# Softmax denominators written into the next pair's score bank, and the packed units' masks made one unit later, in an attention and MLP kernel

## The chip, the cores and the metric

One core of one Trainium2 chip. The metric is the device time of one execution in microseconds; lower is better. The core's engines run side by side, each with its own queue of instructions in a fixed order: PE (matmul), DVE (vector), ACT (activation), POOL (GpSimd) and SP, which here only issues DMAs. They wait for one another through semaphores.

## The reference, cut to what matters

Attention with a sliding window of 128 keys and 4 sink keys over 4 batches, 8 heads, 768 positions and 64 dimensions a head, then a two-layer MLP over all 3,072 tokens. `n_sink` and `window` come as 64-bit integers, the MLP's weights as 64-bit floats.

```python
scores = scale * np.matmul(q, k.transpose(0, 1, 3, 2))
keep = is_sink | in_window
scores = np.where(keep, scores, -1000000000.0)
scores = scores - np.max(scores, axis=-1, keepdims=True)
a = np.exp(scores)
a = a / (np.sum(a, axis=-1, keepdims=True) + 1e-09)
x = np.matmul(a, v)                      # then heads side by side
h = x @ w_in
out = np.maximum(0.01 * h, h) @ w_out
```

## The kernel before, in words

The tokens are cut into 8 units of 384 (half a batch each). A unit's attention runs by pairs of heads (4 pairs), a pair by blocks of 128 queries (j = 0, 1, 2). The first two units ("native") handle two heads side by side; the other six ("packed") one head at a time, with other masks. The unit's MLP has 16 steps: 12 matmuls into a bank h (`h<-xh,wih` and two more kinds), an activation, then 9 matmuls into three banks o. Each product is made in three parts, from high and low halves: `gh` and `gl` of the activation, `wih`/`wil` and `woh`/`wol` of the weights, `xh`/`xl` of attention's output.

The order of PE's instructions is written by hand: attention is a stream of small pieces, the MLP another, and a table of due pieces interleaves them. The first unit's attention (35 pieces and its start) runs ahead of any MLP work; from then on unit u+1's attention goes between unit u's MLP steps. DVE, ACT, POOL and SP get their order from a list scheduler at build time, which works with its own estimates of time; on the chip the order is fixed, whatever the real times are.

For a native pair, block j does this. PE writes the scores of the two heads into two banks (L296, tiles `s`). DVE takes the masked maximum and writes the shifted scores to SBUF (L308, `pk`, and `negm`); ACT makes the exponentials and their sums (L310, `pk` and `sm`); POOL copies the sink columns (L458, `sk`). Two blocks later PE transposes `pk` into a bank t (L337) and ACT, or DVE for the very first pair, copies it out (L342, `pt`). After three blocks `spread` makes the reciprocals of the sums: DVE adds 1e-9 into spare columns of a score bank (L320), takes the reciprocal out of it (L321), and POOL spreads it over 64 columns (L324, `rb`). Three blocks later (two for the first unit's last pair) `gather` transposes the sinks and `rb` into one bank (L372, L375), which is copied out (L379, `r`); `values` multiplies with V and with the sinks (L392, L398, bank `acc`) and DVE scales the result (L404, `r`). `xh` and `xl` follow (L405, L406).

Score banks: in the first unit the tags s0, s1, o0, o1 go round, so a block's two banks come back two blocks later; from the second unit on only s0 and s1 are left, and every block uses both: the first head's scores go to s0, the second's to s1. A bank is written again only when every reader of its last tile is done, the spare columns' reader included.

The MLP's weights arrive as 64-bit words. For each of the 16 steps DVE decodes an input and an output block with three instructions each (L185, L187, L189, through bank d, tiles `di`/`wi` and `do`/`wo`), ACT rounds it to the high half (L198), POOL subtracts for the low half (L199). The first three steps' weights are decoded during the first unit's attention, the block for step n+3 during step n of the first unit's MLP. In that unit the steps' banks h are the same bank, but for step 1. `wi`, `wo` and two mask tiles (`sel`, `own_rows`) share a ring of three buffers.

`late_masks` (L112) makes the masks that only packed units read, mostly on POOL (L119 to L140), with L136 and L142 on DVE; `whole_limits` (L101) makes the 64-bit limits with three DVE instructions (L106 to L108) that only the last part of the program reads. Before, both are written in the first unit's pair 2, block 0.

Of the kernel before, what the change touches and what calls it, by code (L numbers as in the profile page):

```python
# [147 lines left out]
def fast_path(ctx, tc, cpool, qp, qk, vu, vs, vt, wq, out, ident, lims, wz, negm, wmin, wmax):  # L148
# [68 lines left out]
    def native(u):  # L217
        return u < NATU
# [86 lines left out]
    def soft(u, h, j, w, src, mask, sm):  # L305
        col = (u * H + h) * T + j
        neg = negm[:, col:col + 1]
        anchor[0] = nc.vector.tensor_tensor_reduce(out=w, in0=src, in1=mask, scale=-SCALE, scalar=3.0e38,  # L308
                                                   op0=ALU.add, op1=ALU.min, accum_out=neg)
        nc.scalar.activation(out=w, in_=w, func=AF.Exp, scale=-1.0, bias=neg, accum_out=sm)  # L310
# [6 lines left out]
    def spread(u, pair, state, ps):  # L317
        sm = state["sm"]
        rest = ps[:, SPARE:SPARE + 2 * T].rearrange("p (j h) -> p j h", j=T)
        nc.vector.tensor_scalar(out=rest, in0=sm, scalar1=1e-9, scalar2=None, op0=ALU.add)  # L320
        nc.vector.reciprocal(out=sm, in_=rest)  # L321
        rb = xpool.tile([P, TU], F32, tag="rb", name=f"rb{u}_{pair}", bufs=1)
        rb = rb.rearrange("p (c d) -> p c d", c=2 * T)
        nc.gpsimd.tensor_copy(out=rb, in_=sm.rearrange("p j h -> p (j h)").rearrange("p (c o) -> p c o", o=1)  # L324
                              .broadcast_to([P, 2 * T, D]))
        state["rb"] = rb
# [90 lines left out]
        return (u, pair + 1) if pair < NPAIR - 1 else (u + 1, 0)  # L417

    count = [0]

    def attend(u, pair, pend):
        state = {"sk": sks[pair % 2]}
        nxt = ahead(u, pair)

        def later(lag, f, join=False):
            pend.append((count[0] + lag, f, join))

        def fetch(o):
            more = nxt[0] < NU
            if native(u) and native(nxt[0]) and nxt not in raws:  # L430
                load_pair(*nxt)
            if more and o == 0:
                load_values(*nxt)
            if not native(u) and o == 0:
                load_head(u, 2 * pair + 1)
            elif more and not native(nxt[0]):
                load_head(nxt[0], 2 * nxt[1])

        def tile_pt():
            if "pt" not in state:  # L440
                state["pt"] = apool.tile([P, 2, 2 * TU], F32, tag="pt", name=f"pt{u}_{pair}", bufs=1)

        def pt_then(f, *args):
            tile_pt()
            f(*args)

        if native(u):
            state["sm"] = apool.tile([P, T, 2], F32, tag="sm", name=f"sm{u}_{pair}")
            sp = raws.pop((u, pair))
            for j in range(T):  # L450
                kn = KSL[u % 2][j][1]
                pss = scores(u, pair, j, (0, 1), sp)
                w = apool.tile([P, 2, W3], F32, tag="pk", name=f"pk{u}_{pair}_{j}", bufs=3)
                a = P if kn == W3 else 0
                for o, ps in enumerate(pss):
                    soft(u, 2 * pair + o, j, w[:, o, 0:kn], ps[:, 0:kn], masks[min(T * (u % 2) + j, 2)],
                         state["sm"][:, j, o:o + 1])
                    nc.gpsimd.tensor_copy(out=state["sk"][:, 0, j, o, :], in_=w[:, o, a:a + NSK])  # L458
                if j == 0:
                    fetch(0)  # L460
                    if native(nxt[0]):
                        load_sinks(*nxt)
                    if u == 0 and pair == 0:
                        rest(anchor[0])
                    if u == 0 and pair == 2:
                        whole_lim.append(whole_limits(tc, cpool, lim_raw, lim_lo, anchor[0]))
                        late.append(late_masks(tc, cpool, iopool, masks, anchor[0]))
                count[0] += 1
                if j == T - 1:
                    spread(u, pair, state, pss[1])  # L470
                later(LAGT, lambda j=j, w=w: pt_then(turn_native, u, pair, j, w, state))
                yield
        else:
            for o in range(2):
                h = 2 * pair + o
                sp = split_head(u, h)
                fetch(o)
                (split_sinks if o else load_sinks)(u, pair)
                w = apool.tile([P, 2 * W3], F32, tag="pk", name=f"pk{u}_{h}", bufs=3)
                w = w[:, 0:T * W1].rearrange("p (j k) -> p j k", j=T)  # L480
                sm = apool.tile([P, T], F32, tag="sm", name=f"sm{u}_{h}")
                for j in range(T):
                    ps, = scores(u, pair, j, (o,), sp)
                    if KSL[u % 2][j][1] == W3:
                        nc.vector.copy_predicated(out=ps[:, W1:W3], mask=late[0][1], data=ps[:, 0:P])  # L485
                        src = ps[:, P:W3]
                    else:
                        src = ps[:, 0:W1]
                    soft(u, h, j, w[:, j], src, late[0][0][min(T * (u % 2) + j, 2)], sm[:, j:j + 1])
                    count[0] += 1  # L490
                    if j == T - 1:
                        nc.vector.tensor_scalar(out=sm, in0=sm, scalar1=1e-9, scalar2=None, op0=ALU.add)
                        nc.vector.reciprocal(out=sm, in_=sm)
                        nc.vector.tensor_tensor(out=w, in0=w, in1=sm.rearrange("p (j o) -> p j o", o=1)
                                                .broadcast_to([P, T, W1]), op=ALU.mult)
                        sk, sinks = state["sk"], w[:, :, 0:NSK]
                        nc.gpsimd.tensor_copy(out=sk[:, 0:3:2, 0:T, o, :].bitcast(F32R),
                                              in_=sinks.rearrange("p (r j) s -> p r j s", r=1)
                                              .broadcast_to([P, 2, T, NSK]))
                        nc.gpsimd.tensor_tensor(out=sk[:, 1, 0:T, o, :], in0=sinks, in1=sk[:, 0, 0:T, o, :],  # L500
                                                op=ALU.subtract)
                        later(LAGT, lambda o=o, w=w: pt_then(turn_packed, u, pair, o, w, state))
                    yield
        last = u == 0 and pair == NPAIR - 1
        if native(u):
            later(LAGT if last else LAGG, lambda: gather(u, pair, state))
        later(LAGT if last else LAGV if native(u) else LAGP, lambda: values(u, pair, state), not native(u))
# [125 lines left out]
    for x, _ in enumerate(mlp_stream()):  # L633
        u, r = divmod(x, mlp_steps)
# [216 lines left out]
```

## Time and profile before

| what | value |
|---|---|
| median of 3 runs | 702.59 us (701.48 to 704.52) |
| the profiled execution | 702.91 us, span 701.1 us |
| PE busy | 687.3 us, 98% of the span |
| DVE busy | 446.1 us, 64% |
| POOL busy | 321.0 us, 46% |
| ACT busy | 318.8 us, 45% |
| chain that ended last | PE 93%, DVE 3%, DMA 1%, ACT 1% |
| granted clock of PE | 0.999 |

The busy shares are averages over unlike stretches: the first 37 us hold the first unit's attention alone, and the MLP fills PE from then on. [...]

### The profile page before, as it was taken

How to read it: one execution, taken by the hardware profiler on the slowest of the kernel's cores; microseconds unless marked ns; L12 is line 12 of the kernel's file. 1: busy time of each engine (PE TensorE's matmuls, PEld its weight loads, DVE VectorE, ACT ScalarE, POOL GpSimd, SP SyncE). 2: the span in 40 equal slices, each digit the busy share in tenths (PEclk: the TensorE clock that was granted, in tenths of full speed). 3: DMA queues.
4: the chain of work that ended last, by engine and by line, in shares of the span. 5: the costliest groups of instructions: out<-in, count | busy, mean ns of one | idle time of the engine just before them, and what ended most of it. 6: DMA issues, size and time to landing. Idle time of an engine off the chain costs nothing.

```text
span 701.1 us, 11524 instructions
## 1 busy us (share of the span) xinstructions
PE 687.3 (98%) x3950; PEld 597.8 (85%) x3950; DVE 446.1 (64%) x1183; ACT 318.8 (45%) x827; POOL 321.0 (46%) x442
## 2 busy tenths in 40 slices
PE   8899999999999999999999999999999999999996
PEld 5577788988888988888898888888888889889995
DVE  5997887655656665565566565556566565377772
ACT  4865566444454444444444444444444444222221
POOL 4676688544444543543444454354344444122220
PEclk9999999999999999999999999999999999999999
DMA  6666556222123111222113221221222320068751
GB/s 223 207 223 197 192 204 202 82 66 69 47 72 108 56 43 61 60 85 69 58 53 106 70 57 47 62 91 44 67 73 53 110 74 33 1 218 277 252 169 48
DMA packets 29535, 74.14 MB, mean 106 GB/s; under 512 B 3488, under 2 KB 9120, under 8 KB 29472
## 3 DMA queue, kind: packets, MB, share of 16 engines
q1 hardware_dynamic: 29184, 73.10, 32.0%
q8 instruction: 32, 0.52, 0.3%
q14 instruction: 31, 0.25, 0.1%
q10 hardware_dynamic: 288, 0.26, 0.1%
HBM read 67.06 MB, written 6.29 MB: 105 GB/s over the span
## 4 chain that ended last, share of the span: by engine, by line
PE 93%; DVE 3%; DMA 1%; ACT 1%; issue 0%; SPq 0%; ACTq 0%; DVEq 0%
PE h L549 38%; PE o L586 37%; PE acc L392 6%; PE s L301 5%; PE t L348 3%; PE s L296 2%; PE t L337 1%; DVE pk L308 1%; DMA qkraw<-in_qk 1%; PE acc L398 1%; DMA qkn<-in_qp 1%; PE acc L388 1%; PE t L350 0%; ACT pk L310 0%; DVE ob L599 0%
## 5 line engine op out<-in xcount | busy, mean ns | idle before, releaser
L568 POOL TENSOR_TENSOR gl<-g,gh 128x384 fp32r<-128x384 f32 x127 | 129.9, 1023 | 276.2 <-ACT gh L567 260.8
L549 PE MATMUL h<-xh,wih 128*128 128x384 f32 x512 | 180.8, 353 | 0.0
L549 PE MATMUL h<-xl,wih 128*128 128x384 f32 x512 | 172.7, 337 | 0.0
L549 PE MATMUL h<-xh,wil 128*128 128x384 f32 x512 | 172.7, 337 | 0.0
L586 PE MATMUL o<-woh,gh 128*128 128x512 f32 (+1 forms) x400 | 153.5, 385 | 0.2 <-DVE ob L599 0.2
L586 PE MATMUL o<-wol,gh 128*128 128x512 f32 (+1 forms) x400 | 152.8, 385 | 0.0
L310 ACT ACTIVATE pk<-pk,negm 128x132 f32<-128x132 f32 (+1 forms) x192 | 81.6, 426 | 96.7 <-DVE negm L308 96.3
L559 ACT ACTIVATE g<-h 128x384 f32<-128x384 f32 x127 | 62.0, 488 | 123.7 <-PE h L549 103.4
L586 PE MATMUL o<-woh,gl 128*128 128x512 f32 (+1 forms) x400 | 113.8, 387 | 0.0
L549 PEld LDWEIGHTS h<-xh,wih 128*128 128x128 f32 x512 | 96.4, 188 | 4.0 <-issue 2.2
L549 PEld LDWEIGHTS h<-xl,wih 128*128 128x128 f32 x512 | 96.6, 189 | 0.4 <-POOL xl L406 0.2
L549 PEld LDWEIGHTS h<-xh,wil 128*128 128x128 f32 x512 | 96.1, 188 | 0.0
L567 ACT CAST gh<-g 128x384 fp32r<-128x384 f32 x128 | 65.7, 513 | 65.4 <-DVE g L566 64.8
L566 DVE TENSOR_TENSOR g<-h,g 128x384 f32<-128x384 f32 x127 | 69.9, 550 | 35.0 <-ACT g L559 34.9
L586 PEld LDWEIGHTS o<-woh,gl 128*128 128x128 f32 x400 | 74.0, 188 | 17.1 <-POOL gl L568 0.4
L586 PEld LDWEIGHTS o<-woh,gh 128*128 128x128 f32 x400 | 75.1, 188 | 12.0 <-DVE ob L599 0.9
L586 PEld LDWEIGHTS o<-wol,gh 128*128 128x128 f32 x400 | 75.1, 188 | 11.0
L485 DVE COPY_PREDICATED s<-tri,s 128x128 f32<-128x128 int8 x120 | 35.0, 292 | 53.8 <-PE s L301 51.9
L262 POOL TENSOR_TENSOR qksp<-qkraw,qksp 64x396 fp32r<-64x396 f32 (+1 forms) x48 | 56.4, 1176 | 23.1 <-POOL gl L568 18.6
L301 PEld LDWEIGHTS s<-qksp 128*128 128x128 f32 x288 | 53.5, 188 | 8.6
L301 PE MATMUL s<-qksp 128*128 128x260 f32 (+1 forms) x288 | 56.3, 277 | 0.0
L261 ACT CAST qksp<-qkraw 128x780 fp32r<-128x780 f32 (+1 forms) x48 | 43.2, 901 | 25.2 <-PE s L301 22.2
(114 smaller groups left out, 853.8 us busy)
## 6 DMA issues: line engine op xcount, KB each, us to landing
craw<-in_wq SPq DMA_DIRECT2D x32, 512.0 KB, 4.1
qkraw<-in_qk SPq DMA_DIRECT2D x24, 454.0 KB, 3.2
qkraw<-in_qk SPq DMA_DIRECT2D x24, 390.0 KB, 3.0
wiraw<-in_wq SPq DMA_DIRECT2D x16, 512.0 KB, 4.2
woraw<-in_wq SPq DMA_DIRECT2D x16, 512.0 KB, 3.7
out<-ob SPq DMA_DIRECT2D x23, 256.0 KB, 2.0
v<-in_vu SPq DMA_DIRECT2D x16, 256.0 KB, 2.6
v<-in_vu SPq DMA_DIRECT2D x16, 192.0 KB, 2.4
```

What stands on the lines that cost most here:

```text
L261: nc.scalar.copy(out=sp[:, 0:TU + n], in_=raw[:, 0:TU + n])
L262: nc.gpsimd.tensor_tensor(out=sp[D:P, TU:TU + n], in0=raw[D:P, TU:TU + n], in1=sp[D:P, TU:TU + n].bitcast(F32), op=ALU.subtract)
L301: nc.tensor.matmul(pss[0][:, 0:kn], lhsT=sp[:, off + j * P:off + (j + 1) * P], rhs=sp[:, TU + k0:TU + k0 + kn], start=c == 0, stop=c == 1)
L310: nc.scalar.activation(out=w, in_=w, func=AF.Exp, scale=-1.0, bias=neg, accum_out=sm)
L392: nc.tensor.matmul(acc[o * D:(o + 1) * D, qo:qo + m], lhsT=vv[:, kb * P + o * D:kb * P + (o + 1) * D], rhs=state["pt"][:, o, po:po + m], s ...
L485: nc.vector.copy_predicated(out=ps[:, W1:W3], mask=late[0][1], data=ps[:, 0:P])
L549: nc.tensor.matmul(ph[:, 0:TU], lhsT=w[:, cs], rhs=x, start=cc == 0 and c == 0, stop=cc == NCC - 1 and c == 2)
L559: nc.scalar.mul(g, ph[:, 0:TU], 0.01)
L566: anchor[0] = nc.vector.tensor_tensor(out=g, in0=ph[:, 0:TU], in1=g, op=ALU.max)
L567: nc.scalar.copy(out=gh, in_=g)
L568: (nc.vector if step == NU * NFC - 1 else nc.gpsimd).tensor_tensor(out=gl, in0=g, in1=gh.bitcast(F32), op=ALU.subtract)
L586: nc.tensor.matmul(acc, lhsT=(gl if c == 2 else gh)[:, t * P:(t + 1) * P], rhs=(wl if c == 1 else wh)[:, cols], start=f == 0 and c == 0, s ...
```

## The change

`spread` is no longer run when a native pair's last block is written. It waits in a list, and the next pair's block 0 runs it after its own maxima, with its own second bank for the spare columns (or, behind the second unit, the first packed head's first bank). `whole_limits` and `late_masks` are written in the second unit's pair 1, block 0.

```diff
--- before.py
+++ after.py
@@ -417,6 +417,7 @@
         return (u, pair + 1) if pair < NPAIR - 1 else (u + 1, 0)
 
     count = [0]
+    waiting = []
 
     def attend(u, pair, pend):
         state = {"sk": sks[pair % 2]}
@@ -457,17 +458,19 @@
                          state["sm"][:, j, o:o + 1])
                     nc.gpsimd.tensor_copy(out=state["sk"][:, 0, j, o, :], in_=w[:, o, a:a + NSK])
                 if j == 0:
+                    if waiting:
+                        waiting.pop()(pss[1])
                     fetch(0)
                     if native(nxt[0]):
                         load_sinks(*nxt)
                     if u == 0 and pair == 0:
                         rest(anchor[0])
-                    if u == 0 and pair == 2:
+                    if u == 1 and pair == 1:
                         whole_lim.append(whole_limits(tc, cpool, lim_raw, lim_lo, anchor[0]))
                         late.append(late_masks(tc, cpool, iopool, masks, anchor[0]))
                 count[0] += 1
                 if j == T - 1:
-                    spread(u, pair, state, pss[1])
+                    waiting.append(lambda ps: spread(u, pair, state, ps))
                 later(LAGT, lambda j=j, w=w: pt_then(turn_native, u, pair, j, w, state))
                 yield
         else:
@@ -487,6 +490,8 @@
                     else:
                         src = ps[:, 0:W1]
                     soft(u, h, j, w[:, j], src, late[0][0][min(T * (u % 2) + j, 2)], sm[:, j:j + 1])
+                    if waiting:
+                        waiting.pop()(ps)
                     count[0] += 1
                     if j == T - 1:
                         nc.vector.tensor_scalar(out=sm, in0=sm, scalar1=1e-9, scalar2=None, op0=ALU.add)
```

The program's order on PE is the same instruction for instruction up to the branch that is not taken. On the others it moves, since the scheduler lays them out anew. Three places follow. In the names, `pk_p_j` is pair p, block j; `s_h_j` head h, block j; the unit's number is left out, the last number only counts tiles. A matmul or DVE step on two heads has two rows, and `negm` is the second half of each L308.

First place, DVE, first unit, pair 1, block 1. Before:

```order
L308 ISA pk_1_1_221,negm<-s_2_1_217,m_95 128x260
L308 ISA negm 128x1
L320 TENSOR_SCALAR s_1_2_168<-sm_0_134 128x6
L321 RECIPROCAL sm_0_134<-s_1_2_168 128x6
L308 ISA pk_1_1_221,negm<-s_3_1_218,m_95 128x260
L308 ISA negm 128x1
```

After:

```order
L308 ISA pk_1_1_221,negm<-s_2_1_217,m_95 128x260
L308 ISA negm 128x1
L320 TENSOR_SCALAR s_3_0_186<-sm_0_134 128x6
L308 ISA pk_1_1_221,negm<-s_3_1_218,m_95 128x260
L308 ISA negm 128x1
L321 RECIPROCAL sm_0_134<-s_3_0_186 128x6
```

The sum and reciprocal of pair 0 stood in bank `s_1_2` (tag s1), which `s_3_1` writes next; they now stand in `s_3_0` (tag o1), which `s_3_2` writes next, and the reciprocal has gone behind the second head's maximum.

Second place, DVE, second unit, pair 0, block 1. Before:

```order
L185 TENSOR_SCALAR di_516<-wiraw_511 128x512
L308 ISA pk_0_1_555,negm<-s_0_1_551,m_96 128x260
L308 ISA negm 128x1
L187 SCALAR_TENSOR_TENSOR di_516<-wiraw_511,di_516 128x512
L308 ISA pk_0_1_555,negm<-s_1_1_552,m_96 128x260
L308 ISA negm 128x1
L189 SCALAR_TENSOR_TENSOR wi_515<-wiraw_511,di_516 128x512
L404 TENSOR_TENSOR r_3_574<-acc_3_576,r_3_574 128x384
```

After, from the second head of block 0 on:

```order
L308 ISA pk_0_0_468,negm<-s_1_0_465,m_96 128x260
L308 ISA negm 128x1
L185 TENSOR_SCALAR di_490<-wiraw_485 128x512
L320 TENSOR_SCALAR s_1_0_465<-sm_3_356 128x6
L308 ISA pk_0_1_529,negm<-s_0_1_525,m_96 128x260
L308 ISA negm 128x1
L187 SCALAR_TENSOR_TENSOR di_490<-wiraw_485,di_490 128x512
L321 RECIPROCAL sm_3_356<-s_1_0_465 128x6
L189 SCALAR_TENSOR_TENSOR wi_489<-wiraw_485,di_490 128x512
L308 ISA pk_0_1_529,negm<-s_1_1_526,m_96 128x260
L308 ISA negm 128x1
L404 TENSOR_TENSOR r_3_548<-acc_3_550,r_3_548 128x384
```

The first unit's last pair's sum now stands in `s_1_0` (tag s1), which `s_1_1` writes next, and its reciprocal stands behind the first head's maximum and a decode step.

The same place on ACT. Before:

```order
L310 ACTIVATE pk_0_0_498,sm_0_493<-pk_0_0_498,negm 128x260
L310 ACTIVATE pk_0_1_555,sm_0_493<-pk_0_1_555,negm 128x260
L342 COPY pt_3_534<-t_3_2_562 128x2x256
L379 COPY r_3_574<-sk_3_569 128x512
L310 ACTIVATE pk_0_1_555,sm_0_493<-pk_0_1_555,negm 128x260
L198 CAST wih_547<-wi_515 128x512
```

After:

```order
L310 ACTIVATE pk_0_0_468,sm_0_463<-pk_0_0_468,negm 128x260
L310 ACTIVATE pk_0_1_529,sm_0_463<-pk_0_1_529,negm 128x260
L198 CAST wih_521<-wi_489 128x512
L342 COPY pt_3_508<-t_3_2_536 128x2x256
L310 ACTIVATE pk_0_1_529,sm_0_463<-pk_0_1_529,negm 128x260
L379 COPY r_3_548<-sk_3_543 128x512
```

The cast of `wi` (step 2's input weights) has moved ahead of the copy of `t_3_2`, the last piece of `pt` that `acc_3` reads.

Third place, DVE, around the activation of the first MLP step. Before:

```order
L185 TENSOR_SCALAR di_619<-wiraw_614 128x512
L321 RECIPROCAL sm_0_493<-s_1_2_600 128x6
L187 SCALAR_TENSOR_TENSOR di_619<-wiraw_614,di_619 128x512
L566 TENSOR_TENSOR g_0_641<-h_0_628,g_0_641 128x384
L189 SCALAR_TENSOR_TENSOR wi_618<-wiraw_614,di_619 128x512
```

After (L571 is L566 of before):

```order
L189 SCALAR_TENSOR_TENSOR wo_564<-woraw_487,do_565 128x512
L185 TENSOR_SCALAR di_589<-wiraw_584 128x512
L187 SCALAR_TENSOR_TENSOR di_589<-wiraw_584,di_589 128x512
L189 SCALAR_TENSOR_TENSOR wi_588<-wiraw_584,di_589 128x512
L571 TENSOR_TENSOR g_0_611<-h_0_598,g_0_611 128x384
```

The activation `g_0` has moved behind the last decode step of `wi` (step 3's input weights).

The same place on POOL. Before:

```order
L199 TENSOR_TENSOR wol_596<-wo_590,woh_595 128x512
L324 COPY rb_0_612<-sm_0_493 128x384
L568 TENSOR_TENSOR gl_0_643<-g_0_641,gh_0_642 128x384
L199 TENSOR_TENSOR wil_646<-wi_618,wih_645 128x512
L458 COPY sk_105<-pk_1_0_692 128x4 x2
```

After (L573 and L459 are L568 and L458 of before):

```order
L199 TENSOR_TENSOR wol_570<-wo_564,woh_569 128x512
L199 TENSOR_TENSOR wil_616<-wi_588,wih_615 128x512
L573 TENSOR_TENSOR gl_0_613<-g_0_611,gh_0_612 128x384
L459 COPY sk_105<-pk_1_0_662 128x4
L199 TENSOR_TENSOR wol_620<-wo_593,woh_619 128x512
```

`gl_0` has moved behind `wil` of step 3, and pair 0's `rb_0` no longer stands ahead of it.

## Rows read from the trace of the kernel before

**Rows 1.** Busy time of each engine by stretch; the first line names the columns.

```profile
core 0: us, PE busy (x) PEld busy (x) DVE busy (x) ACT busy (x) POOL busy (x), PEclk, DMA share, GB/s
0.00:36.80 36.80, 32.10 (x210) 20.22 (x210) 27.16 (x102) 23.66 (x74) 20.88 (x67) 1.00 0.64 215
36.80:80.80 44.00, 43.32 (x249) 34.19 (x250) 39.60 (x89) 27.65 (x67) 31.57 (x41) 1.00 0.62 206
...
120.00:701.10 581.10, 574.02 (x3279) 511.40 (x3279) 346.31 (x923) 241.55 (x628) 237.01 (x302) 1.00 0.27 85
```

**Rows 2.** The chain that ended last: start us, length us, what.

```profile
10.93 0.21 DVE sm L321
...
17.36 0.40 DVE pm L142 x2
...
23.18 0.17 DVE s L320
```

**Rows 3.** Timeline of PE: start us, length us, engine, line, operation; [idle before, releaser].

```profile
9.54 0.70 PE L296 MATMUL s<-qkn 64*128 64x260 f32 x2
11.18 0.70 PE L296 MATMUL s<-qkn 64*128 64x260 f32 x2 [0.95 <-DVE sm L321]
11.82 0.66 PE L337 MATMUL t<-ident,pk 128*128 128x128 f32 x4
...
12.51 0.71 PE L296 MATMUL s<-qkn 64*128 64x260 f32 x4
...
31.77 0.71 PE L296 MATMUL s<-qkn 64*128 64x260 f32 x4
...
34.22 1.30 PE L392 MATMUL acc<-pt,v 128*64 128x256 f32 x12 [0.61 <-ACT pt L342]
...
36.73 0.44 PE L549 MATMUL h<-xh,wih 128*128 128x384 f32 x1
...
43.05 0.50 PE L586 MATMUL o<-woh,gl 128*128 128x512 f32 x1
...
51.42 0.45 PE L549 MATMUL h<-xh,wih 128*128 128x384 f32 x1
```

**Rows 4.** Timeline of DVE, same columns.

```profile
10.38 0.43 DVE L308 CUSTOM_DVE_ANT_0 pk<-s,m 128x260 f32<-128x260 f32 x1
...
16.14 0.56 DVE L404 TENSOR_TENSOR r<-acc,r 128x384 f32<-128x384 f32 x1 [0.78 <-PE acc L398]
...
18.28 0.87 DVE L107 SCALAR_TENSOR_TENSOR lim_hi<-lim_lo,lim_hi 128x2 f32<-128x2 f32 x1
...
20.02 0.15 DVE L108 SCALAR_TENSOR_TENSOR lim<-lim_hi,lim_lo 128x2 f32<-128x2 f32 x1
...
30.50 0.52 DVE L404 TENSOR_TENSOR r<-acc,r 128x384 f32<-128x384 f32 x1
...
36.26 0.56 DVE L404 TENSOR_TENSOR r<-acc,r 128x384 f32<-128x384 f32 x1 [1.66 <-PE acc L398]
36.74 0.68 DVE L185 TENSOR_SCALAR do<-woraw 128x512 int32<-128x512 int32 x1
...
40.20 0.69 DVE L187 SCALAR_TENSOR_TENSOR di<-wiraw,di 128x512 int32<-128x512 int32 x1
...
50.03 0.55 DVE L566 TENSOR_TENSOR g<-h,g 128x384 f32<-128x384 f32 x1
```

**Rows 5.** Timeline of ACT, same columns.

```profile
33.60 0.56 ACT L342 COPY pt<-t 128x512 f32<-128x512 f32 x1
...
41.98 0.62 ACT L198 CAST wih<-wi 128x512 fp32r<-128x512 f32 x1
```

**Rows 6.** Timeline of POOL, same columns.

```profile
4.68 0.35 POOL L125 TENSOR_SCALAR_AFFINE_SELECT low<-low 128x128 f32<-128x128 f32 x1
...
18.14 1.00 POOL L406 TENSOR_TENSOR xl<-r,xh 128x384 fp32r<-128x384 f32 x1
...
41.98 1.02 POOL L568 TENSOR_TENSOR gl<-g,gh 128x384 fp32r<-128x384 f32 x1
42.95 1.30 POOL L199 TENSOR_TENSOR wil<-wi,wih 128x512 fp32r<-128x512 f32 x1
```


## The prediction

> **What bounds the kernel now.** I read the stretches first [rows 1]. From 36.8 us on PE is never short of work: busy 574.02 of 581.10 us after 120 us, and 43.32 of 44.00 just after the MLP begins. A change to waits is worth something only where PE stands: ahead of 36.8 us, where it is busy 32.10 of 36.80 us. So the question is when the first MLP matmul starts, now 36.73 us [rows 3], and whether PE is let through afterwards: in 36.8 to 80.8 us DVE is busy 39.60 of 44.00 us and POOL 31.57 [rows 1], so what feeds the MLP there has little room. Next I read the chain of waits: the reciprocal L321 is on it at 10.93, the mask step L142 at 17.36 for 0.40, the sum L320 at 23.18 [rows 2]. All three are things that the change moves.
>
> **The change, part by part.** No work is added or taken out, so the whole effect is in order and waits. I follow the path on the clock of the profiled execution.
>
> *1. Pair 1, block 1: a gain.* Before, the second head's scores wait for the reciprocal in their bank: `s_2_1` goes alone at 9.54, `s_3_1` follows at 11.18 after an idle 0.95, and the transposes come 0.64 later at 11.82. Side by side both heads take 0.71 us, as at 12.51 [rows 3]. With the bank free the transposes could come at 9.54 + 0.64 = 10.18, which is 1.64 earlier. Part is given back at once: the reciprocal now sits in the bank of `s_3_2`. Its DVE place is behind two maxima that start at 10.38 and take 0.35 each (0.43 long, with the overlap of 0.08 that 36.26 and 36.74 show for an instruction of 0.56) [rows 4] and the sum, so it starts near 11.2. PE gets through 0.25 after such a start (10.93 to 11.18) [rows 2, 3], at 11.45 instead of 10.95. What stays is 1.64 - 0.5 = 1.1 us, and the L404 of 16.14 [rows 4] should start near 15.05.
>
> *2. The masks leave the first unit: a gain, partly stopped by ACT.* On DVE the six moved instructions (L106, L136, two L142, L107, L108) stood between the L404 of 16.14 and the next. The two L142 put 0.40 on the chain [rows 2], L107 is 0.87 long [rows 4], the other three are no longer than L108's 0.15 or a little over; about 1.5 us in all. The sum also no longer makes DVE wait for exponentials, as at 23.18 [rows 2]. Were all of that to arrive, the L404 of 30.50 [rows 4] would come 1.1 + 1.5 = 2.6 earlier; if none did, 1.1. ACT lies between: it now copies `r` behind both exponentials of the pair's last block, so PE's L398 waits for it. I take 1.8: 28.7. POOL's six mask instructions (none longer than L125's 0.35 [rows 6]) stood in its first 6 us, off the path, and cost nothing there; POOL is busy 20.88 of the first 36.80 us [rows 1].
>
> *3. Second unit, pair 0, block 1: most of it is given back.* Only s0 and s1 are left here, and the reciprocal of the last pair sits in s1, which this block's second head wants. From L404 to the scores is 30.50 to 31.77 [rows 3, 4], 1.27, so the first head starts at 29.97, alone, 0.70 long [rows 3]. DVE reads it at 30.7; behind its 0.35 stands a decode step of 0.61 (0.69 less the overlap [rows 4]) and only then the reciprocal: 31.66. The second head starts 0.25 later at 31.91, the transposes of `t_3_2` 0.64 later at 32.55, their copy 0.66 after that. The cast now ahead of that copy on ACT is done by about 33.0 (0.62 [rows 5] behind a decode that ends near 32.4), so it adds nothing while the bank is this late; without the bank wait the cast alone would hold the copy until then. The copy takes 0.56 [rows 5], so `acc_3` starts at 33.8 against 34.22 [rows 3]. Both the L404 of 36.26 [rows 4] and the first MLP matmul of 36.73 [rows 3] follow it and come 0.4 earlier: 35.85 and 36.3.
>
> *4. The first `gl`: a loss.* Before, `gl` is made at 41.98 to 43.00, ahead of `wil` at 42.95 [rows 6], and PE takes it at 43.05 [rows 3]. Now it stands behind that `wil` on POOL, `wil` needs the cast on ACT, the cast needs the last decode step of `wi` on DVE, and all of DVE's steps there stand behind the L404 in its queue. Before, that decode's middle step starts at 40.20, 3.94 after the L404 of 36.26 [rows 4]; a dependent step follows 0.72 later, 4.66. In the new order a maximum fills one such pause, which saves about 0.13: 35.85 + 4.53 = 40.38, ending 41.06. Then 0.62 for the cast [rows 5], 1.3 for `wil` and 1.02 for `gl` [rows 6], with 0.05 to 0.1 between engines: `gl` is ready at 44.05, PE takes it at 44.1. Against 43.05 this is a loss of **1.05**. Queued behind the waiting matmul are the rest of that output block and every later PE piece, so the loss goes to the end: PE's idle time up to 80.8 us is 0.7 in all [rows 1], too little to take it back.
>
> *5. The masks in the second unit.* DVE's instructions now stand ahead of step 1's activation. What hides them is the distance to PE's next need: the activation of step 2 at 50.03 [rows 4] must have read its bank before step 3 writes it at 51.42 [rows 3]. The same walk gives an end of that activation at 52.2 and PE at 51.42 + 1.05 = 52.47, hidden by 0.1 to 0.3. That counts L107 at 0.87, and L108 at its 0.15 [rows 4], its price with POOL idle. At L107's price L108 costs 0.72 more; 0.4 to 0.6 of it would reach PE. As it starts within 0.1 us of the `gl` of step 1, I cannot tell which; I take the low value and keep both. POOL's six, 2.1 us at most, lie behind `gl` of step 1 and ahead of that of step 2, which PE asks for only when step 3's twelve matmuls are through.
>
> L107 shows why the price is open: it runs 18.28 to 19.15 beside a POOL subtraction of 18.14 to 19.14 and ends with it [rows 4, 6]. [...]
>
> The change in the third unit (the packed sinks' load is now asked for earlier, the last `rb` of the second unit later) lies where PE has no waits [rows 1]; I cost it at nothing, and if that cover went it would cost what `gather` waited.
>
> **Sum.** -1.1 - 0.7 + 1.4 (back) + 1.45 (`gl` against the 0.4 kept) = +1.05. The profiled execution took 702.91 us (span 701.1 and 1.8 around it), so 703.96; it lies 0.32 above the median of 702.59, and on that median the change gives 703.6 to 703.7.
>
> **Rivals.**
> - *The gain arrives (faster).* If the bank wait of part 3 is absent or short (the reciprocal gets done while the first head still runs, below 0.2 us of wait), the L404 of 36.26 comes up to 1.8 earlier. Then `gl` is ready at 34.46 + 8.2 = 42.65: 0.4 earlier than before, 702.2. Were `gl` also in time (the decode of `wi` would have to end by 39.6 - 1.4 = 38.2), the whole 1.8 is kept: 700.8. For it: ACT and DVE durations are steady. Against: the order has the decode step between maximum and reciprocal, and `wil` ahead of `gl`, whatever the times.
> - *A second stop at step 3.* If L108 waits out the `gl` of step 1, or the L142 meet POOL too, step 2's activation ends up to 1 us after step 3 wants the bank. Loss 1.05 + 0.6 to 1.0: 704.2 to 704.7. For it: L107's row; DVE's 39.60 of 44.00 us. Against: POOL waits for ACT in much of that stretch.
> - *It changes nothing.* The walk's errors cancel the gain and the loss, within 0.4 us: 702.2 to 703.0. For it: each of the two is a sum of ten durations. Against: parts 1 and 4 rest on order alone.
>
> **How the numbers follow.** Forecast, a loss of 0.5 to 1.5: 0.47. Second stop: 0.2. Nothing: 0.13. The gain arrives: 0.13. Something larger: 0.07, of which 0.05 slower, since stops between DVE and POOL could add up in that stretch, and 0.02 faster. All but the last lie inside 0.5% (3.5 us, about what a measurement of this kernel can tell from no change): 0.93 for the same. Predicted: 703.7. The range goes from half of the first rival's gain to the second's upper price and the spread of the runs: 701.3 to 705.5; the forecast alone 703.0 to 704.2.
>
> **What would show it.** Part 1: the two heads' scores side by side near 9.5, an idle of some 0.5 before `s_3_2`. Part 2: L404s near 15.05 and 28.7. Part 3: a PE wait for L321 near 31, `h` starting near 36.3. Part 4: PE idle for 1.4 to 1.7 before the first `gl`, released by POOL L573, near 44.1. Part 5: L107 long again, and `h` of step 3 without a wait. The prediction is wrong if the first `gl` is on time, or if PE waits a second time before 60 us.

## The result, and the profile after the change

The changed kernel takes 707.36 us in the median of 9 executions (706.27 to 712.54), the kernel before 702.57 in the 9 that ran beside it (one of them, of 1356.57 us, is a slow run and stays out of the ratio); the ratio is 1.0068, with a 95% interval of 1.0047 to 1.0090. That is slower by 0.7%, and outside the range of the prediction. The profiled execution took 707.36 us, its span is 705.6 us against 701.1: 4.5 us more. All ratios below are to the kernel before, run on the same chip as the kernel they stand for.

First the stretches of the changed kernel, in the columns of [rows 1]:

```profile
core 0: us, PE busy (x) PEld busy (x) DVE busy (x) ACT busy (x) POOL busy (x), PEclk, DMA share, GB/s
28.00:33.00 5.00, 3.05 (x16) 1.85 (x16) 4.12 (x13) 3.49 (x10) 3.48 (x9) 1.00 0.72 262
33.00:37.00 4.00, 4.00 (x23) 2.77 (x21) 0.54 (x3) 2.27 (x5) 1.98 (x4) 0.57 0.41 131
37.00:46.25 9.25, 7.90 (x46) 5.84 (x42) 8.11 (x20) 5.03 (x13) 4.97 (x7) 1.00 0.62 194
46.50:50.50 4.00, 4.00 (x14) 3.31 (x14) 3.96 (x11) 1.91 (x5) 2.89 (x4) 0.57 0.43 138
50.50:80.80 30.30, 29.62 (x168) 23.36 (x167) 24.78 (x57) 18.25 (x47) 20.10 (x32) 1.00 0.51 182
```

The column to read is PEclk. Before the change it is 1.00 in every stretch of [rows 1]. Here it is 0.57 twice, over 4 us each. Read in slices of 0.5 us it is 0.50 in every slice from 33.5 to 36.5 us and from 47.0 to 50.0, which is the half clock spoken of below; PE was busy in all of both stretches. What it did ahead of each fall is in PE's timeline of the changed kernel:

```profile
9.49 0.71 PE L296 MATMUL s<-qkn 64*128 64x260 f32 x4
...
10.82 1.23 PE L296 MATMUL s<-qkn 64*128 64x260 f32 x4
...
30.48 0.70 PE L296 MATMUL s<-qkn 64*128 64x260 f32 x2
32.53 0.70 PE L296 MATMUL s<-qkn 64*128 64x260 f32 x2 [1.34 <-DVE sm L321]
33.16 1.12 PE L337 MATMUL t<-ident,pk 128*128 128x128 f32 x4
...
35.28 1.92 PE L392 MATMUL acc<-pt,v 128*64 128x256 f32 x12
...
38.40 0.44 PE L554 MATMUL h<-xh,wih 128*128 128x384 f32 x1
...
44.35 0.50 PE L591 MATMUL o<-woh,gh 128*128 128x512 f32 x1 [0.18 <-ACT gh L572]
...
46.25 0.50 PE L591 MATMUL o<-woh,gl 128*128 128x512 f32 x1 [1.18 <-POOL gl L573]
...
49.68 0.67 PE L554 MATMUL h<-xh,wih 128*128 128x384 f32 x1
...
56.19 0.44 PE L554 MATMUL h<-xh,wih 128*128 128x384 f32 x1
```

Ahead of the first fall it waited 1.34 us for the reciprocal L321, ahead of the second 0.18 for `gh` and 1.18 for `gl`. Behind the first, four transposes take 1.12 us and the `acc` matmuls 1.92, where [rows 3] have 0.66 and 1.30 for the same work. Then the queues that PE waited for, DVE and POOL of the changed kernel:

```profile
14.97 0.56 DVE L404 TENSOR_TENSOR r<-acc,r 128x384 f32<-128x384 f32 x1 [1.60 <-PE acc L398]
...
29.18 0.56 DVE L404 TENSOR_TENSOR r<-acc,r 128x384 f32<-128x384 f32 x1 [0.64 <-PE acc L398]
...
32.29 0.19 DVE L321 RECIPROCAL sm<-s 128x6 f32<-128x6 f32 x1
...
37.94 0.56 DVE L404 TENSOR_TENSOR r<-acc,r 128x384 f32<-128x384 f32 x1 [4.23 <-PE acc L398]
...
47.37 0.95 DVE L107 SCALAR_TENSOR_TENSOR lim_hi<-lim_lo,lim_hi 128x2 f32<-128x2 f32 x1
```

```profile
43.96 1.28 POOL L199 TENSOR_TENSOR wil<-wi,wih 128x512 fp32r<-128x512 f32 x1 [0.96 <-ACT wih L198]
45.19 1.01 POOL L573 TENSOR_TENSOR gl<-g,gh 128x384 fp32r<-128x384 f32 x1
```

The L404s that [rows 4] have at 16.14, 30.50 and 36.26 stand at 14.97, 29.18 and 37.94; the last has waited 4.23 us for PE. On POOL `gl` stands behind `wil`, where [rows 6] have it ahead.

### The profile page after: what moved, and what is told of

Its sections match the earlier page's. It is cut to its first block, busy times and chain, and to the rows that moved or that the text cites. A ratio compares the mean times of both kernels' runs of the same rounds, so it can differ in the third digit from the quotient of the medians.

```text
span 705.6 us, 11539 instructions
## 1 busy us (share of the span) xinstructions
PE 690.8 (98%) x3950; PEld 600.0 (85%) x3950; DVE 446.2 (63%) x1183; ACT 319.1 (45%) x827; POOL 320.3 (45%) x442
## 4 chain that ended last, share of the span: by engine, by line
PE 94%; DVE 2%; ACT 2%; DMA 1%; issue 1%; POOL 0%; DVEq 0%; POOLq 0%; ACTq 0%
PE h L554 37%; PE o L591 37%; PE acc L392 6%; PE s L301 5%; PE t L348 3%; PE s L296 2%; PE t L337 2%; PE acc L398 1%; PE warm L272 1%; DMA qkraw<-in_qk 1%; ACT pk L310 1%; PE acc L388 0%; PE t L350 0%; DVE ob L604 0%; PE sk L375 0%
## 5 line engine op out<-in xcount | busy, mean ns | idle before, releaser
L573 POOL TENSOR_TENSOR gl<-g,gh 128x384 fp32r<-128x384 f32 x127 | 129.6, 1021 | 276.3 <-ACT gh L572 260.0
L571 DVE TENSOR_TENSOR g<-h,g 128x384 f32<-128x384 f32 x127 | 69.9, 550 | 32.2 <-ACT g L564 31.9
```

What stands on the lines that cost most here:

```text
L571: anchor[0] = nc.vector.tensor_tensor(out=g, in0=ph[:, 0:TU], in1=g, op=ALU.max)
L573: (nc.vector if step == NU * NFC - 1 else nc.gpsimd).tensor_tensor(out=gl, in0=g, in1=gh.bitcast(F32), op=ALU.subtract)
```

## The experiments

The theory after the two traces: the order costs about what the prediction gave for it, and the rest is the clock, which falls behind each of the two PE waits. Rival 1: the waits and the order cost it all, the half clock only goes with them. Rival 2: the masks' work in the second unit costs it, not the denominators.

**Fill the first wait (fill_first).** In `scores`, ahead of the second head's matmuls:

```diff
+                if o and (u, pair, j) == (1, 0, 1):
+                    keep_warm(7)
```

`keep_warm(n)` is the kernel's own helper: n bfloat16 matmuls on zeros into a bank of their own. The order on DVE, ACT and POOL is that of the change.

> The changed kernel, with seven extra bfloat16 matmuls on zeros between the two heads' scores of the second unit's pair 0, block 1, where PE stood idle for 1.34 us. They depend on nothing that is late and add about 0.8 us of PE work inside that wait; the order on DVE and POOL stays. Clock theory (each of the two PE waits is followed by about 3.3 us at half clock, which costs some 1.7 us each, and the walk's own loss is 1.05): the granted clock stays near 1.00 from 33 to 37 us, the L404 of 37.94 starts near 36.2, and the second wait with its fall stays: 705.7 us against 707.4. Rival 1 (the waits themselves and the order cost it all, the clock is incidental): nothing is won, the L404 stays at 37.9, 707.4. Rival 2 (the masks' work in the second unit costs it): 707.4.

Ratio 1.0012 (0.9993 to 1.0031), span 701.8. Timeline of PE (lines are 2 higher than in the changed kernel) and two stretches:

```profile
30.66 0.70 PE L298 MATMUL s<-qkn 64*128 64x260 f32 x2
31.30 0.94 PE L272 MATMUL warm<-wz 128*128 128x256 bf16 x7
32.71 0.70 PE L298 MATMUL s<-qkn 64*128 64x260 f32 x2 [0.47 <-DVE sm L323]
...
37.18 0.45 PE L556 MATMUL h<-xh,wih 128*128 128x384 f32 x1
...
45.04 0.50 PE L593 MATMUL o<-woh,gl 128*128 128x512 f32 x1 [1.17 <-POOL gl L575]
```

```profile
33.00:37.00 4.00, 3.87 (x31) 2.54 (x30) 1.00 (x4) 2.18 (x5) 2.11 (x5) 1.00 0.44 137
...
45.00:50.00 5.00, 4.96 (x27) 4.02 (x28) 4.93 (x15) 2.86 (x7) 3.67 (x6) 1.00 0.41 122
```

The second head starts 2.05 us after the first, exactly as in the changed kernel: the seven matmuls have shortened no one's wait for anything. But the clock stays at 1.00, and from the first head's start to the first `gl` matmul it takes 14.38 us instead of 15.77. Rival 1 is out. More was won than the theory gave: the wait of 1.17 us for `gl` is still there, and here no fall stands behind it. The mean clock, which is the granted clock averaged over the span, was 0.997 or more in 9 of 12 executions; in the changed kernel it was 0.996 or less in all 9. (A profiled execution without half clock behind a wait has 0.997 to 0.999, since the end of a span, without work on PE, can be at half clock: 0.50 in 700.0 to 701.1 us of the kernel before, 0.52 in 702.0 to 705.6 of the changed one.)

**Fill the second wait (fill_second).** In the output matmuls, ahead of the first that reads `gl`:

```diff
+                    if step == 1 and n == 2:
+                        keep_warm(10, bank("h", "warm2"))
```

> The changed kernel, with ten extra bfloat16 matmuls on zeros, in another bank, ahead of the first matmul of step 1 that reads gl, where PE stood idle for 1.18 us. The order on POOL and DVE up to that matmul stays; behind it a few instructions change places. Clock theory: the granted clock stays near 1.00 from 46 to 50 us, the matmul of gl still starts near 46.2, but the activations and scores behind it come about 1.7 us sooner (h of step 1 near 48.0 instead of 49.7): 705.7 us; the fall at 33 to 37 stays. Rival 1 (waits and order alone): 707.4 or a little over. Rival 2 (masks): 707.4.

Ratio 1.0031 (1.0012 to 1.0050), span 704.2. The two stretches that were at 0.57:

```profile
33.00:37.00 4.00, 4.00 (x19) 2.71 (x20) 0.80 (x3) 2.27 (x5) 2.24 (x5) 0.57 0.41 131
46.50:50.50 4.00, 4.00 (x22) 3.39 (x24) 3.96 (x14) 2.20 (x7) 2.72 (x4) 1.00 0.40 137
```

In this execution, the fastest of its 12, the first fall stays and the second is gone; the mean clock is 0.996 or less in all 12. The ratio lies between those of the change and `fill_first`, as the clock theory has it, but its interval touches both, and 705.7 us was expected (a ratio of 1.0045). `h` of step 3 meets a wait of 0.31 us on an activation that the changed kernel didn't have.

**Both filled (fill_both).** The two edits together.

> The changed kernel with both waits filled: seven extra bfloat16 matmuls on zeros between the two heads' scores of the second unit's pair 0, block 1, and ten ahead of the first matmul of step 1 that reads gl. No order changes ahead of that matmul. Clock theory: no stretch at half clock behind either wait, the order's own loss stays (in fill_first the matmul of gl came 2.0 us later than before the change), mean clock 0.997 or more in nearly all executions: ratio to before 1.000 to 1.002. Rival 1 (waits and order alone): 1.0068, as for the change without the fillings. Rival 2 (masks): 1.0068.

Ratio 1.0017 (1.0001 to 1.0032), mean clock 0.997 or more in 11 of 12. As expected, and no better than the first filling alone. Its profiled execution also shows a wait of 1.18 us for a DMA (`qkn<-in_qp`) ahead of the scores of the first unit's pair 2, block 0, which start at 13.52. In the changed kernel they start at 12.57 without a wait, in the kernel before at 13.74: part 1's gain has brought them close to that transfer, and in some executions it is late (0.21 us in `fill_second`, 0.46 in `own_bank`, 1.44 in `denoms_only`).

**A part of the first wait filled (fill_third).** `keep_warm(3)` in place of `keep_warm(7)`; a wait of 0.91 us is left.

> The changed kernel with three extra bfloat16 matmuls instead of seven between the two heads' scores of the second unit's pair 0, block 1, so that some 0.95 us of the 1.34 us of wait stay, as long as the wait of the kernel before at 10 us. If the length of a wait decides whether the clock falls, and 1.34 us always and 0.95 us rarely does it: ratio near that of fill_first, 1.001 to 1.002, with few executions under 0.997. If any wait of about a microsecond can do it: between fill_first and the change, 1.003 to 1.005, with executions of both kinds. If seven matmuls helped by something other than the shorter wait (their mere number): near the change, 1.0068.

Ratio 1.0023 (1.0005 to 1.0042). The executions are of both kinds: six at a mean clock of 0.997 or more (704.07 to 706.14 us) and six at 0.995 or less (706.25 to 707.47). The profiled one is of the second kind (lines 2 higher):

```profile
32.29 0.93 PE L298 MATMUL s<-qkn 64*128 64x260 f32 x2 [0.91 <-DVE sm L323]
```

```profile
32.00:36.00 4.00, 3.71 (x15) 2.55 (x17) 1.29 (x5) 2.44 (x7) 2.74 (x5) 0.58 0.44 145
```

So a wait of 0.91 us can do it too, in some executions. In this one the clock falls behind the wait of 1.18 us for `gl` as well (0.57 in 46 to 50 us). The two kinds of execution bear out the second reading, though the ratio lies a little under the 1.003 to 1.005 that it gave; the third, at 1.0068, is outside the interval.

**`gl` ahead of `wil` again (gl_first), and with the first wait filled (fill_gl).**

```diff
-                if u == 0 and new < NFC:
+                if u == 0 and new < NFC and step:
                     round_weights(new)
...
+                if u == 0 and new < NFC and not step:
+                    round_weights(new, after=made)
```

`made` is the subtraction that makes `gl`; in step 0 that of `wil` is issued behind it. A few steps of unit 2 change places too.

> The changed kernel with one order undone: on POOL the first gl stands ahead of the wil of the same stretch again, as before the change. gl follows its gh at about 44.4 and is ready at 45.4; PE wants it at 45.07, so 0.3 to 0.4 us of wait stays instead of 1.18. Clock theory: 0.8 us of the wait is won, and if so short a stop doesn't lower the clock 1.7 us more: 704.9 us; if the clock falls all the same, 706.6. Rival 1 (waits alone): 706.6, with the clock's fall still there or not. Rival 2 (masks): 707.4.

> The changed kernel with the first wait filled by seven extra bfloat16 matmuls on zeros, and the first gl ahead of the wil of the same stretch on POOL. Clock theory: no half clock at 33 to 37 us; the wait for gl shrinks from 1.17 us to about 0.35, so the first gl comes some 1.2 us later than before the change instead of 2.0: ratio 0.9995 to 1.001, some 0.8 us below fill_first. Rival 1 (waits alone): the two waits have lost 0.8 of about 2.5 us, ratio 1.005. Rival 2 (masks): 1.0068.

`gl_first`: 1.0053 (1.0031 to 1.0075). The wait for `gl` shrank from 1.18 to 0.35 us and the profiled execution has no second fall (span 703.7), but that execution is the second fastest of the 12 and the median is not clearly below the change's: 1.0053 is 706.3 us on the 702.57 of before, near the 706.6 of rival 1 and of a clock that falls all the same. The timing doesn't settle it, and its mean clocks go from 0.982 to 0.997. `fill_gl`: 1.0012 (0.9994 to 1.0029), mean clock 0.997 or more in 11 of 12. Its `gl` matmul starts at 44.06 us, 1.0 earlier than in `fill_first`, and PE's last matmul 1.3 earlier (694.34 against 695.61); the span is only 0.2 shorter (701.6), because the way from PE's last matmul to the end of the span is longer here. In the medians nothing of it shows.

**Denominators alone (denoms_only).**

```diff
-                    if u == 1 and pair == 1:
+                    if u == 0 and pair == 2:
```

> One part of the change alone: the denominators sit in the next pair's first bank, the late masks and the limits are made in the first unit as before. gl stands ahead of wil on POOL here. Clock theory: the wait between the heads' scores of the second unit's pair 0, block 1 is there and the clock falls behind it, so the L404 of 36.26 before comes near 38.5 and the first gl 6.8 later, at 45.3 instead of 43.05: 704.5 to 705 us. Rival 1 (waits alone, no price of the clock): L404 near 36.9, 703.1 to 703.4. Rival 2 (it is the masks' work in the second unit that costs): no slower than before, 701.5 to 702.6.

Ratio 1.0055 (1.0036 to 1.0075), mean clock 0.993 or less in all 9. PE and stretches:

```profile
13.76 0.50 PE L296 MATMUL s<-qkn 64*128 64x132 f32 x4 [1.44 <-DMA qkn<-in_qp]
...
20.67 0.70 PE L296 MATMUL s<-qkn 64*128 64x260 f32 x2 [1.10 <-ACT pt L342]
...
22.69 2.40 PE L392 MATMUL acc<-pt,v 128*64 128x256 f32 x12
...
36.32 1.23 PE L296 MATMUL s<-qkn 64*128 64x260 f32 x2 [1.34 <-DVE sm L321]
```

and DVE:

```profile
20.43 0.18 DVE L321 RECIPROCAL sm<-s 128x6 f32<-128x6 f32 x1
```

```profile
10.00:20.00 10.00, 7.86 (x52) 4.71 (x50) 6.75 (x27) 4.74 (x18) 3.43 (x11) 1.00 0.43 142
21.50:25.00 3.50, 3.50 (x20) 1.96 (x18) 2.43 (x6) 2.34 (x7) 1.85 (x4) 0.54 0.76 230
36.50:42.50 6.00, 6.00 (x26) 3.87 (x27) 0.82 (x3) 2.27 (x5) 2.27 (x5) 0.52 0.28 90
```

The loss is there without the masks' move: rival 2 is out as the cause. The size was off, since a second place lost the clock: in this order the second head of pair 2's block 2 waits 1.10 us, and the clock falls there as well. The row names a copy of ACT, which ended at the same time, but a score bank has no part in that copy. What this head needs is the bank of `s_5_0`, and pair 1's reciprocal came out of it only at 20.43, behind L107 (0.85 us), a decode step and two maxima; the score follows 0.24 later, as behind the other L321s. So it is the wait of part 1's new bank, made long by the limits' and decode work in the same queue. The fall behind the wait of 1.34 is longer than in the changed kernel: from that score to the first MLP matmul it's 7.02 us (36.32 to 43.34), against 5.87 there and 4.47 in `fill_first`. The DMA wait of 1.44 us at 12.3, on the other hand, has no fall behind it.

**Masks alone (masks_only).** The other edits of the diff undone.

> The other part of the change alone: the late masks and the limits are made in the second unit, the denominators stay in their own pair's bank as before. Clock theory: no new wait and no new fall; the wait of 1.05 us near 23.4 shrinks and the first MLP matmul starts 0.7 to 1.1 us earlier: 701.5 to 702.6 us, ratio 0.998 to 1.000. Rival 1 (waits alone): the same. Rival 2 (the masks' work in the second unit costs it): 1.004 to 1.007.

Ratio 1.0015 (0.9995 to 1.0034), which decides nothing about a few tenths of a per cent. PE's timeline shows why it isn't faster:

```profile
36.02 0.44 PE L549 MATMUL h<-xh,wih 128*128 128x384 f32 x1
...
51.28 0.44 PE L549 MATMUL h<-xh,wih 128*128 128x384 f32 x1 [0.36 <-DVE g L566]
...
57.25 0.44 PE L549 MATMUL h<-xh,wih 128*128 128x384 f32 x1 [0.44 <-DVE g L566]
```

The first MLP matmul is 0.71 us earlier than in [rows 3], as expected. Then PE waits 0.36 and 0.44 us for activations that DVE makes too late: it is busy almost without a pause from 42.2 us on, the masks and limits among its work, and the activation of step 2 starts at 50.67 instead of 50.03. That is a stop where the prediction's rival had one, but not by its cause: L108 took 0.15 us and the two L142 0.49 together; L107 took 0.99. PE's last matmul starts at 693.87, before the change at 693.90, so the gain is gone by then. In the changed kernel's order on DVE there is no such stop: `h` of step 3 starts without a wait at 56.19, and in `fill_first` at 53.39.

**The last pair of the first unit in its own bank (own_bank).** This keeps the change but for the pair behind which only two score banks are left:

```diff
-                    waiting.append(lambda ps: spread(u, pair, state, ps))
+                    if u == 0 and pair == NPAIR - 1:
+                        spread(u, pair, state, pss[1])
+                    else:
+                        waiting.append(lambda ps: spread(u, pair, state, ps))
```

It also moves `gl` back ahead of `wil` on POOL.

> The changed kernel, but the denominators of the first unit's last pair are made at once in that pair's own bank, as before the change; all other pairs keep the next pair's bank, and the masks are made in the second unit. On POOL gl stands ahead of wil here. Clock theory: no wait between the two heads' scores of the second unit's pair 0, block 1, so no fall of the clock; the gains of the first unit reach the first MLP matmul, near 35.2 us instead of 36.73, and gl is not late. The wait near 87 us (1.37 before) may take some of it back: 700.5 to 702 us, ratio 0.997 to 0.999. Rival 1 (waits alone): the same, 0.997 to 0.999. Rival 2 (the masks' work in the second unit costs it): 1.003 or more.

Ratio 0.9979 (0.9958 to 0.9999), mean clock 0.997 or more in 11 of 12. Its PE timeline:

```profile
30.75 0.71 PE L296 MATMUL s<-qkn 64*128 64x260 f32 x4
...
35.71 0.45 PE L557 MATMUL h<-xh,wih 128*128 128x384 f32 x1
...
42.10 0.50 PE L594 MATMUL o<-woh,gl 128*128 128x512 f32 x1
```

Both heads run side by side, no wait, and the first MLP matmul starts 1.02 us earlier than in [rows 3] (1.5 was expected; 0.46 went to the DMA wait named above). This is faster than the change, and barely clear of the kernel before. Most of the gain over the kernel before goes with the clock: the medians on this chip are 701.94 and 703.61, 1.7 us apart, but among executions at a mean clock of 0.997 or more (11 of 12, and 14 of 35) they are 701.91 and 702.34, 0.4 apart. The change takes away the kernel before's wait of 0.95 us and leaves 0.57 and 0.24 of that of 1.05, and here no long bank wait comes in their place. Denominators, masks and POOL's order move together, so it doesn't price them one by one.

**The same fillings in the kernel before (before_fill), and that kernel profiled again (before_again, before_again2).** Seven matmuls in each of the two waits of the first unit, order unchanged. One wait is in [rows 3]; the other is the second row here, from the kernel before, and the first row is needed further down:

```profile
16.84 0.63 PE L337 MATMUL t<-ident,pk 128*128 128x128 f32 x4 [0.26 <-DVE r L404]
...
24.46 0.66 PE L337 MATMUL t<-ident,pk 128*128 128x128 f32 x4 [1.05 <-DVE r L404]
```

The edit:

```diff
+                if o and (u, pair, j) == (0, 1, 1):
+                    keep_warm(7)
...
-            keep_warm(1)
+            keep_warm(8 if (pair, j) == (2, 0) else 1)
```

> The kernel before the change with its two waits of the first unit filled: seven extra bfloat16 matmuls on zeros between the two heads' scores of pair 1, block 1 (idle 0.95 us) and seven more behind the transposes of pair 2, block 0 (idle 1.05 us). The order on DVE, ACT and POOL stays. Clock theory: a wait of about 1 us is followed by half clock in some executions and not in others; of the 67 executions of the kernel before on two chips 37 had a mean clock of 0.995 or less. With the waits filled most executions have 0.997 or more, and the ratio to before is 0.997 to 0.9985, though no wait of DVE or ACT has become shorter. Rival (the low clock of those executions has nothing to do with these waits): ratio 1.000, and the same share of executions at 0.995 or less.

> The kernel before, unchanged, profiled once more. Clock theory: if this execution has a mean clock of 0.995 or less, the half clock stands right behind one of its waits of about a microsecond (10.2, 23.4 or 86.1 us), and the span is some 1.7 us longer for each. Rival: the half clock stands where PE had no wait.

> As before_again, another execution: the half clock, if there is any, stands behind a wait of about a microsecond by the clock theory, elsewhere by the rival.

`before_fill`: 0.9966 (0.9950 to 0.9982). Its first MLP matmul starts at 36.70 us against 36.73: so neither the reciprocal nor the L404 that PE waits for comes more than 0.04 us sooner, and the gain is not in the order. Of its 11 executions 10 had a mean clock of 0.997 or more and one 0.996, while 51 of the 89 executions of the kernel before that ran beside these experiments had 0.995 or less. (Part of the gain isn't accounted for by this: among executions at 0.997 or more, 10 here and 7 of the kernel before on this chip, the medians still differ by 1.1 us.) `before_again2` has no half clock (702.66 us). `before_again` (706.46 us) has it, and this is where:

```profile
9.57 0.70 PE L296 MATMUL s<-qkn 64*128 64x260 f32 x2
11.22 1.15 PE L296 MATMUL s<-qkn 64*128 64x260 f32 x2 [0.95 <-DVE sm L321]
...
19.99 0.63 PE L337 MATMUL t<-ident,pk 128*128 128x128 f32 x4 [0.26 <-DVE r L404]
```

```profile
5.00:11.00 6.00, 4.59 (x26) 2.65 (x26) 4.82 (x27) 3.87 (x17) 2.80 (x16) 1.00 1.03 376
...
11.00:18.00 7.00, 6.78 (x27) 3.91 (x29) 3.10 (x11) 2.20 (x8) 1.74 (x7) 0.52 0.39 123
20.00:30.00 10.00, 8.95 (x63) 5.67 (x63) 9.90 (x38) 7.72 (x25) 6.04 (x15) 1.00 0.61 195
```

The wait of 0.95 us is that of [rows 3], in place and length. There the clock stayed at 1.00; here the half clock begins with the very matmul that ends the wait. The other two waits of about 1 us have none behind them in this execution. This one fall is dear: the transposes of 19.99 come 8.77 us after the matmul that ends the wait, and in the profiled kernel before 5.66 (11.18 to 16.84). That is 3.1 us, where 1.7 was expected for each fall; the span is 3.5 longer.

## Why the prediction was wrong

Points of the path, in us of the profiled executions (the prediction's own column is what its text gives; its end is the span of before and 1.05):

| | before | predicted | changed | fill_first | own_bank |
|---|---|---|---|---|---|
| second unit, pair 0, block 1: first head | 31.77 | 29.97 | 30.48 | 30.66 | 30.75 |
| first MLP matmul | 36.73 | 36.3 | 38.40 | 37.18 | 35.71 |
| first `gl` matmul | 43.05 | 44.1 | 46.25 | 45.04 | 42.10 |
| transposes behind the wait of 0.68 | 64.94 | | 69.70 | 66.91 | 63.96 |
| transposes behind the next wait | 87.46 | | 91.95 | 88.57 | 86.44 |
| start of PE's last matmul | 693.90 | | 698.43 | 695.61 | 693.41 |
| end of the span | 701.1 | 702.15 | 705.6 | 701.8 | 700.5 |

*Part 1 was right.* The two heads stand side by side at 9.49, the idle before `s_3_2` is within the 1.23 us of the group at 10.82 (0.71 without it), and the L404 came at 14.97 for 15.05.

*Part 2 was right in kind, 0.5 short in size.* The L404 came at 29.18 for 28.7. ACT's copy of `r` holds PE's L398 for 0.56 and 0.45 us, more than was allowed for.

*Part 3 found the wait and missed what stands behind it; this is the step that failed.* A wait of 1.3 us was foreseen (29.97 and 0.64 to 31.91), 1.34 came, behind DVE's decode step as the order said. It was priced at its length alone; the clock behind it was put at nothing. From the second head's scores to the first MLP matmul the prediction has 4.4 us (31.91 to 36.3). The changed kernel took 5.87 (32.53 to 38.40), `fill_first`, at full clock, 4.47 (32.71 to 37.18). So the walk was right, and the fall cost 1.4 us on top of the wait; up to the `gl` matmul it's 1.39 (15.77 against 14.38). Even at full clock nothing of the gain was kept: the first MLP matmul of `fill_first` came 0.45 later than before, where 0.4 earlier was predicted. Most of that miss, 0.69, was there when the first head started, from part 2.

*Part 4 was right as a chain and failed in the same way.* L404 to `gl` matmul was taken as 8.2 us; it is 8.31 in the changed kernel and 8.32 in `fill_first`. Idle of 1.4 to 1.7 was foreseen, 0.18 and 1.18 came. At full clock the `gl` matmul is 2.0 us late and not 1.05, because the L404 ahead of it came at 36.72 in `fill_first` and not at 35.85. Behind it the clock fell again: from the `gl` matmul to the transposes of the next pair the changed kernel takes 23.45 us, `fill_first` 21.87, which is 1.58 more.

*Part 5 was right*: L107 is long again (47.37 to 48.32, beside POOL's subtraction `wol` of 47.03 to 48.30), L108 is not: it takes 0.11 at 49.42, where POOL's `gl` of 1.01 us starts too, so the second rival's stop by L108 did not come. And `h` of step 3 starts without a wait, in `fill_first` too, where PE is 2.8 us earlier. `masks_only` shows that another order on DVE does make PE stop there.

*The sum.* The +1.05 for order and waits was too low even without the clock. The spans of single executions hide it, since what follows PE's last matmul takes 6.2 to 7.3 us and differs from run to run. On PE, in the kernel before, the changed one and `fill_first`:

```profile
693.90 0.28 PE L586 MATMUL o<-woh,gl 128*128 128x256 f32 x1
...
698.43 0.28 PE L591 MATMUL o<-woh,gl 128*128 128x256 f32 x1
...
695.61 0.28 PE L593 MATMUL o<-woh,gl 128*128 128x256 f32 x1
```

`fill_first` ends 1.71 us later than before: 2.0 late at `gl`, 1.1 behind the wait near 87 us (which shrank from 1.37 to 0.51, though the kernel before itself has it at 1.02 in `before_again2`), and 0.6 lost again behind that. Its executions say the same: at a mean clock of 0.997 or more the median is 704.38 (9 of 12), that of the kernel before on the same chip 702.45 (13 of 32), 1.9 apart. The ratio of 1.0012 shows less because the median of before holds executions at lower mean clocks, down to 0.987. Between `fill_first` and the changed kernel PE's last matmul moves by 2.82 us: 1.39 and 1.58 for the two falls, less 0.18 by which `fill_first` started the stretch later. The other 1.0 of the 3.8 us between their spans lies behind PE's work. So the 4.5 us of the changed kernel are 1.7 of order and waits, for which 1.05 was predicted, and 2.8 of clock, for which nothing was.

*The rivals.* None had the clock in it. That it stood at 1.00 in every stretch of the one execution that was read said nothing of waits that were yet to come; other executions of the kernel before, at mean clocks down to 0.987, would have been a sign of it, and `before_again` shows half clock behind one of its own waits (0.52 from 11 to 18 us, behind the 0.95).

What stays open: why the wait for `gl` is followed by a fall in the changed kernel and in `fill_third` (1.18 us in both, 0.57 behind it), and at 1.17 us not in the profiled `fill_first` (1.00); in the first two it comes after a first fall, and the runs don't show whether that matters.

## What to carry to other kernels

A wait of PE of about a microsecond can cost more than its length: here 1.4 to 3.1 us more for a fall of the clock behind it, so price it at both ends, with and without. Where such a wait can't be removed, fill it with what fits: in `fill_first` seven matmuls on zeros, 0.94 us in a wait of 1.34, left the second head's start at 2.05 us behind the first, and 9 of 12 executions had a mean clock of 0.997 or more, where none of the changed kernel's 9 had; where a bank is handed on, count the banks left at the place where their number drops. And of a kernel that has such waits, read the mean clock of many executions, not the one trace, and compare two traces at PE's last matmul as well as at the end of the span.

## What the runs showed of the hardware

- Length alone doesn't decide whether the clock falls behind a wait: 0.91 us (`fill_third`), 0.95 (`before_again`) and 1.10 (`denoms_only`) were followed by half clock, 0.95, 1.05 and 1.37 in the profiled kernel before, 1.17 in `fill_first` and 1.44 in `denoms_only` were not. The bank wait of 1.34 us had a fall behind it in all four profiled executions that have it unfilled (the changed kernel, `fill_second`, `gl_first`, `denoms_only`); the wait near 87 us, 1.02 to 1.38 us long in seven, in none. The same wait of 0.95 us in the same program went both ways. Of the three profiled executions of the kernel before, one has a fall behind it (0.52 from 11 to 18 us in `before_again`) and two have none (1.00 in 10 to 20 us); no run here shows the reason.
- Half clock came in busy stretches: in 33 to 37 us of the changed kernel PE was busy 4.00 of 4.00 us at a granted clock of 0.57. In `before_again` it lasted from 11 to 18 us, at 0.52. There it began with the matmul that ends the wait of 0.95 us; from 5 to 11 us the clock had been 1.00.
- Seven matmuls on zeros of 0.94 us in all, at a place where PE would have stood still, were worth some 0.6% (ratio 1.0068 without, 1.0012 with them).
